# Output stage of three chunks with the weights held and 512 rows streamed, on one Trainium2 core

## The chip, the core and the metric

The kernel runs on one core of one Trainium2 chip. The metric is the device time of one launch in microseconds. Engines are named as in the profile: PE is TensorE's matmul stream and PEld its weight loads, DVE is VectorE, ACT ScalarE, POOL GpSimd, SP SyncE, which issues most DMAs.

## What is computed

One sequence of 2048 rows with 640 features, in bfloat16. The rows are normalised, and attention and a gated feed-forward block run side by side on the normalised rows; both are added to the input.

```python
xn = layernorm(x)                       # S=2048, D=640
q, k, v = split(xn @ wqkv)              # 32 heads of 20
s = q k^T * 20**-0.5, kept where 0 <= row - col < 256
o = softmax(s) v
h = sigmoid(xn @ w_gate) * (xn @ w_up)  # F=1536
out = x + o @ wo + h @ w_down
```

## The kernel before

**Tiling.** The rows are cut in four chunks of 512 (`CW`), a chunk into four blocks of 128 rows. Features lie in five groups of 128 (`DC`), the hidden 1536 in twelve (`FC`). Normalised rows are held turned (`xnT`, features on partitions). Gate and up products of a chunk give `h` (twelve tiles of 128 hidden features x 512 rows), attention gives `oc` (five tiles of 128 features x 512 rows).

**Order.** The schedule is by hand: every engine executes its instructions in the order in which the program names them. The main loop (`todo`) walks through 75 attention steps: scores on TensorE into one PSUM buffer of four banks (L504), the exponential on ScalarE (L510), masks on GpSimd (L493) and VectorE (L521), and two steps after the end of a pair the product with `v` (`pv`, L537), whose sums VectorE turns (L548), scales (L558, L563) and turns again into `oc` (L571). Between the steps the object `fill` draws pieces of the dense work from a list of generators: at least 1950 ns of it (`APART`) between two steps, and otherwise so much that a chunk's work is used up by its deadline. Every `yield` gives its nominal cost; most pieces also release one of the queued steps on VectorE (`fill.behind`). The list has, for each chunk, gate and up (`g_gu`, lines L418, L421, L427, L431), the projections (`g_qk`, `g_v`, lines L270, L274, L276, L328) and the output (`g_out`). `norms2` and `norms3` mix the normalising of later chunks in (L211, L230, L247).

**PSUM.** All dense work and `pv` share four banks (`ps_d`, tag "d"), handed out in turn.

**The output stage.** `g_out` runs for chunks 0, 1 and 2. For each block of 128 rows two accumulators take 12 matmuls each over the hidden features (`down`, L441: h is the stationary operand, 320 columns of `wd` stream), and then 5 each over `oc` (`add_wo`, L448). VectorE adds half of the sum to the rows of x (L452, the product with 0.5 because `h` and the ones in `v` carry a factor), and SyncE stores the block (L463). Loads of x (L458) are issued one block ahead into three buffers. Between the first block's `down` and its `add_wo` stands one gate/up group of the next work. Chunk 3's output is not in `g_out` but written out at the end of the kernel, with its four loads of x on ScalarE's queue.

**Neighbours on SyncE's queue.** In chunk 0 the loads of x stand ahead of the turn of chunk 2 (L252, L255), the spreading of q and k (L291) and x of chunk 3 (L118). Behind the stores come the writes of q and k of the next chunk (L278), each of them from one of six `st` buffers.

The weights' columns are taken at a step of five already in the projection of q and k:

```python
wt = wqkv[:, d, base:base + D].rearrange("p (k m) -> p m k", m=DC)
nc.tensor.matmul(ps, lhsT=wt[:, m, :], rhs=xnT[c][:, :, d, :], ...)   # L270
```

Of the kernel before, what the change touches and what calls it, by code (L numbers as in the profile page):

```python
# [9 lines left out]
P = 128  # L10
S = 2048
D = 640
# [3 lines left out]
DC = D // P  # L16
FC = F // P
CW = 512
NCH = S // CW
SBC = CW // P  # L20
HG = 4
# [8 lines left out]
ADD = mybir.AluOpType.add  # L30
MULT = mybir.AluOpType.mult
# [4 lines left out]
BF16 = mybir.dt.bfloat16  # L36
FP32 = mybir.dt.float32
# [32 lines left out]
def kernel(  # L70
# [11 lines left out]
    nc = tc.nc  # L82
    x2 = A_x.flatten_outer_dims()
    out2 = out.flatten_outer_dims()
    xr = x2.rearrange("(n p) d -> p n d", p=P)

    def pool(name, bufs, **kw):
        return ctx.enter_context(tc.tile_pool(name=name, bufs=bufs, **kw))

    const = pool("const", 1)  # L90
    xp = pool("xp", 1)
    lnp = pool("lnp", 4)
# [9 lines left out]
    tp = pool("tp", 2)  # L102
    np_ = pool("np", 1)
    ps_d = pool("ps_d", 4, space=bass.MemoryType.PSUM)
# [6 lines left out]
    xc = {}  # L111
# [12 lines left out]
    wd = const.tile([P, FC, D], BF16, name="wd")  # L124
    wo = const.tile([P, DC, D], BF16, name="wo")
# [208 lines left out]
    MM = 216  # L334
# [47 lines left out]
    def g_qk(c, behind={}):  # L382
        for w in "qk":
            for m in range(DC):
                proj_block(w, c, m)
                behind.get((w, m), lambda: None)()
                yield 5 * MM
        if c:
            spread("q", c, 0, 2)
            spread("k", c, 0, 2)  # L390
        else:
            for r in range(2):
                spread("q", c, r, r + 1)
                spread("k", c, r, r + 1)
                if r == 0:
                    load_gu(wu, B_w_up, 0, FS // 2)
# [11 lines left out]
    ht = {}  # L408
# [5 lines left out]
    def g_gu(c, f0, f1):  # L414
        for f in range(f0, f1):
            pg = ps_d.tile([P, CW], FP32, name="pg", tag="d")
            for d in range(DC):
                nc.tensor.matmul(pg, lhsT=part(wg, d, f), rhs=xnT[c][:, :, d, :],  # L418
                                 start=(d == 0), stop=(d == DC - 1))
            th = tp.tile([P, CW], FP32, name="th")  # L420
            nc.scalar.activation(out=th, in_=pg, func=TANH, scale=0.5)  # L421
            fill.hold = True
            yield 5 * MM
            fill.hold = False
            pu = ps_d.tile([P, CW], FP32, name="pu", tag="d")
            for d in range(DC):
                nc.tensor.matmul(pu, lhsT=part(wu, d, f), rhs=xnT[c][:, :, d, :],  # L427
                                 start=(d == 0), stop=(d == DC - 1))
            h = hp.tile([P, CW], BF16, name="h")
            ht[c, f] = h  # L430
            nc.vector.scalar_tensor_tensor(out=h, in0=th, scalar=1.0, in1=pu, op0=ADD, op1=MULT)  # L431
            yield 5 * MM


    oc = {}

    HALVES = ((0, HALF), (HALF, D))

    def down(c, s, y, cut):
        for f in range(FC):  # L440
            nc.tensor.matmul(y[:, 0:cut[1] - cut[0]], lhsT=ht[c, f][:, s * P:(s + 1) * P],  # L441
                             rhs=wd[:, f, cut[0]:cut[1]], start=(f == 0), stop=False)
            if f % 6 == 5:
                yield 6 * 136

    def add_wo(c, s, y, cut):
        for m in range(DC):
            nc.tensor.matmul(y[:, 0:cut[1] - cut[0]], lhsT=oc[c, m][:, s * P:(s + 1) * P],  # L448
                             rhs=wo[:, m, cut[0]:cut[1]], start=False, stop=(m == DC - 1))

    def add_x(y, cut, rows):
        nc.vector.scalar_tensor_tensor(  # L452
            out=rows[:, cut[0]:cut[1]], in0=y[:, 0:cut[1] - cut[0]], scalar=0.5,
            in1=rows[:, cut[0]:cut[1]], op0=MULT, op1=ADD)

    def new_rows(c, s, name="rows", bufs=3, queue=nc.sync):
        rows = lnp.tile([P, D], BF16, name=name, bufs=bufs)
        queue.dma_start(out=rows, in_=xr[:, c * SBC + s, :])  # L458
        return rows

    def store(c, s, rows, cut=(0, D), queue=nc.sync):
        sb = c * SBC + s
        queue.dma_start(out=out2[sb * P:(sb + 1) * P, cut[0]:cut[1]], in_=rows[:, cut[0]:cut[1]])  # L463

    def outp(c, s, ys, rows):
        for y, cut in zip(ys, HALVES):
            add_wo(c, s, y, cut)
        for y, cut in zip(ys, HALVES):
            add_x(y, cut, rows)
        store(c, s, rows)  # L470

    def g_out(c, between, ahead=()):
        coming = new_rows(c, 0)
        for s in range(SBC):
            rows = coming
            if s < SBC - 1:
                coming = new_rows(c, s + 1)
            if s == 0:
                yield from ahead
            ys = [ps_d.tile([P, CW], FP32, name=f"y{i}", tag="d") for i in range(2)]  # L480
            for y, cut in zip(ys, HALVES):
                yield from down(c, s, y, cut)
            if s == 0:
                yield from between
                fill.flush()
            outp(c, s, ys, rows)
            yield 10 * 136


    def select(part, n, sign):  # L490
# [125 lines left out]
    def mix(a, b, first, every=1, rest=True):  # L616

        for k, cost in enumerate(a):
            yield cost
            if k >= first and (k - first) % every == 0:  # L620
                yield next(b, 0)
        if rest:
            yield from b
# [94 lines left out]

    fill = Fill()
    GU = 10 * MM  # L720
    OUT = 4 * 34 * 136
    APART = 1950
    def later(load, *args):
        load(*args)
        yield 0
# [12 lines left out]
    fill.add("gu0c", mix(g_gu(0, 9, 12), norms2, 0, 1, False), 3 * GU)  # L738
    fill.add("gu1a", mix(g_gu(1, 0, 2), norms2, 0, 1, False), 2 * GU)
    fill.add("out0", mix(g_out(0, g_gu(1, 2, 3)), norms2, 1, 1), OUT + GU)  # L740
    fill.add("qk2", mix(g_qk(2), norms3, 2, 1, False), 50 * MM)
    fill.add("v2", g_v(2), 40 * 136)
    fill.add("gu1b", mix(g_gu(1, 3, 12), norms3, 0, 2), 9 * GU)
    fill.add("turn3", later(turn_rows, 3), 0)
    fill.add("out1", g_out(1, g_gu(2, 0, 1)), OUT + GU)
    fill.add("qk3", g_qk(3), 50 * MM)
    fill.add("v3", g_v(3), 40 * 136)
    fill.add("gu2", g_gu(2, 1, 12), 11 * GU)
    fill.add("out2", g_out(2, (), g_gu(3, 0, 1)), OUT + GU)
    fill.add("gu3", g_gu(3, 1, 12), 11 * GU)  # L750

# [34 lines left out]
    c = NCH - 1  # L786

    def run(gen):
        for _ in gen:
            pass  # L790

    rows = [new_rows(c, s, queue=nc.scalar) for s in range(SBC - 1)]
    rows.append(xp.tile([P, SBC, D], BF16, name="xc")[:, 0, :])
    nc.scalar.dma_start(out=rows[-1], in_=xr[:, S // P - 1, :])
    banks.close()
    ps_y = pool("ps_y", 4, space=bass.MemoryType.PSUM)
    ys = {}
# [53 lines left out]
```

## Time and profile before

| | us |
|---|---|
| median of 3 runs | 308.99 |
| lowest, highest | 308.94, 309.14 |
| profiled execution | 309.52 |
| span of that execution, first to last instruction | 307.2 |
| TensorE busy in it | 303.1 (99%) |
| ScalarE | 193.1 (63%) |
| VectorE | 184.2 (60%) |
| GpSimd | 83.4 (27%) |

The span is what the views of the profile cover; the time of the execution is longer by what lies around it. "Busy" counts an engine's instructions from start to end; matmuls are pipelined, so TensorE's share says that it is occupied, not that each of its cycles does work. The granted TensorE clock is 1.0 all through. The page has parts for busy time, for 40 slices of the span, for DMA queues, for the chain of work that ended last, and for groups of instructions. In a group's line stand: code line, engine, operation, out<-in, shape, count | busy us, mean ns of one | idle us of the engine before them, and what ended it.

### The profile page before, as it was taken

Reading aid. Unit: us, or ns where it says so; the run is one execution under the profiler, and the core shown is the slowest. Engines: PE = TensorE matmul, PEld = TensorE weight load, DVE = VectorE, ACT = ScalarE, POOL = GpSimd, SP = SyncE. Lnnn points to the kernel's source line nnn. Section 1 sums busy time; section 2 is a strip of 40 time slices with the busy share of each in tenths; the row PEclk is TensorE's granted clock in tenths of the full one; section 3 lists DMA queues with packets and bytes.
Section 4 is the critical chain, followed back from the end, with each engine's and each line's share of the span. In section 5 each row is a group of like instructions: output and inputs, shape, how many; then the busy total and the mean of one; then the engine's idle time right before and its main releaser. Section 6 shows DMA issues by size and latency. Waiting matters only on the chain.

```text
span 307.2 us, 10157 instructions
## 1 busy us (share of the span) xinstructions
PE 303.1 (99%) x4434; PEld 168.4 (55%) x4434; DVE 184.2 (60%) x378; ACT 193.1 (63%) x183; POOL 83.4 (27%) x189
## 2 busy tenths in 40 slices
PE   8999999999999999999999999999999999999996
PEld 3654445564556655654556655644546665444774
DVE  5777449298984489487642666354383627464523
ACT  6923795977766458867656557768765466778000
POOL 5011234635314123512213132341314132221100
PEclk9999999999999999999999999999999999999999
DMA  7998899789029522721052022550000210000301
GB/s 215 346 279 258 278 266 317 212 251 220 5 81 274 151 78 99 216 81 66 23 128 87 25 76 88 182 173 2 3 2 5 69 39 23 2 2 2 89 21 64
DMA packets 35756, 36.86 MB, mean 120 GB/s; under 512 B 2944, under 2 KB 35456, under 8 KB 35712
## 3 DMA queue, kind: packets, MB, share of 16 engines
q1 hardware_dynamic: 34304, 33.84, 37.2%
q0 software_dynamic: 544, 1.61, 1.7%
q10 hardware_dynamic: 864, 0.77, 0.9%
q8 instruction: 34, 0.56, 0.7%
q14 instruction: 10, 0.08, 0.1%
HBM read 25.59 MB, written 11.44 MB: 121 GB/s over the span
## 4 chain that ended last, share of the span: by engine, by line
PE 97%; DMA 1%; ACT 0%; DVE 0%; SPq 0%; issue 0%
PE pg L418 18%; PE y L441 18%; PE pu L427 17%; PE pqk L270 15%; PE ps L504 9%; PE y L448 7%; PE acc L537 6%; PE pv L328 6%; PE pv L308 1%; DMA xc<-in_A_x_dram 1%; PE pt L236 0%; PE pvh L308 0%; ACT turn L644 0%; PE pwarm L200 0%; DVE turn L230 0%; SPq L135 0%
## 5 line engine op out<-in xcount | busy, mean ns | idle before, releaser
L510 ACT ACTIVATE pT<-ps 128x2048 bf16<-128x2048 f32 x75 | 140.8, 1877 | 55.2 <-PE ps L504 32.6
L493 POOL TENSOR_SCALAR_AFFINE_SELECT pT<-pT 64x256 bf16<-64x256 bf16 (+1 forms) x126 | 67.2, 533 | 180.2 <-ACT pT L510 122.1
L418 PE MATMUL pg<-xnT,wg 128*128 128x512 bf16 x240 | 59.9, 380 | 0.0
L427 PE MATMUL pu<-xnT,wu 128*128 128x512 bf16 x240 | 59.8, 380 | 0.0
L431 DVE SCALAR_TENSOR_TENSOR h<-th,pu 128x512 bf16<-128x512 f32 x48 | 32.8, 684 | 42.4 <-ACT th L421 25.7
L441 PE MATMUL y<-wd,h 128*128 128x320 bf16 (+2 forms) x396 | 56.8, 295 | 0.0
L270 PE MATMUL pqk<-xnT,wqkv 128*128 128x512 bf16 x200 | 45.8, 381 | 0.0
L441 PEld LDWEIGHTS <-h 128*128 128x128 bf16 x396 | 36.8, 98 | 15.9 <-issue 2.3
L521 DVE TENSOR_TENSOR pT<-pT,keep 128x512 bf16<-128x512 bf16 (+2 forms) x81 | 35.5, 445 | 15.3 <-ACT pT L510 14.4
L421 ACT ACTIVATE th<-pg 128x512 f32<-128x512 f32 x48 | 28.6, 595 | 20.2 <-PE pg L418 19.9
L427 PEld LDWEIGHTS <-wu 128*128 128x128 bf16 x240 | 22.3, 98 | 27.3 <-issue 2.0
L418 PEld LDWEIGHTS <-wg 128*128 128x128 bf16 x240 | 21.7, 98 | 26.4 <-issue 3.0
L270 PEld LDWEIGHTS <-wqkv 128*128 128x128 bf16 x200 | 22.6, 119 | 19.0 <-issue 1.5
L504 PE MATMUL ps<-qT,kT 20*64 20x320 bf16 (+4 forms) x1440 | 32.0, 260 | 0.0
L548 DVE STREAM_TRANSPOSE t<-acc 128x512 f32<-128x512 f32 x32 | 21.0, 694 | 17.8 <-PE acc L537 17.8
L452 DVE SCALAR_TENSOR_TENSOR rows<-y,rows 128x320 bf16<-128x320 f32 x30 | 14.2, 488 | 25.2 <-PE y L448 20.4
L504 PEld LDWEIGHTS <-kT 20*64 20x64 bf16 x1440 | 13.5, 103 | 27.2 <-issue 27.1
L448 PE MATMUL y<-wo,oc 128*128 128x320 bf16 (+2 forms) x165 | 24.2, 295 | 0.0
L537 PE MATMUL acc<-pT,v 64*32 64x320 bf16 (+4 forms) x1440 | 20.0, 253 | 0.0
L448 PEld LDWEIGHTS <-oc 128*128 128x128 bf16 x165 | 15.5, 98 | 6.7 <-issue 1.0
L537 PEld LDWEIGHTS <-v 64*32 64x32 bf16 x1440 | 17.0, 92 | 3.4 <-issue 0.9
L328 PE MATMUL pv<-wqkv,xnT 128*64 128x320 bf16 x240 | 17.4, 300 | 0.0
(61 smaller groups left out, 174.1 us busy)
## 6 DMA issues: line engine op xcount, KB each, us to landing
qT<-sq SPq DMA_DIRECT2D x16, 256.0 KB, 4.4
kT<-sk SPq DMA_DIRECT2D x16, 256.0 KB, 4.3
xc<-in_A_x_dram SPq DMA_DIRECT2D x16, 160.0 KB, 4.3
sq<-st SPq DMA_DIRECT2D x20, 128.0 KB, 3.7
sk<-st SPq DMA_DIRECT2D x20, 128.0 KB, 2.8
out_dram<-rows SPq DMA_DIRECT2D x15, 160.0 KB, 1.8
wg<-in_B_w_gate_dram SPq DMA_DIRECT2D x4, 480.0 KB, 7.7
wu<-in_B_w_up_dram SPq DMA_DIRECT2D x4, 480.0 KB, 6.8
```

Source lines behind the costliest of these rows:

```text
L270: nc.tensor.matmul(ps, lhsT=wt[:, m, :], rhs=xnT[c][:, :, d, :], start=(d == 0), stop=(d == DC - 1))
L328: nc.tensor.matmul(ps[hf * U:(hf + 1) * U, 0:HALF], lhsT=xnT[c][:, s, d, rows], rhs=wqkv[:, d, 2 * D + hf * HALF:2 * D + (hf + 1) * HALF], ...
L418: nc.tensor.matmul(pg, lhsT=part(wg, d, f), rhs=xnT[c][:, :, d, :], start=(d == 0), stop=(d == DC - 1))
L427: nc.tensor.matmul(pu, lhsT=part(wu, d, f), rhs=xnT[c][:, :, d, :], start=(d == 0), stop=(d == DC - 1))
L431: nc.vector.scalar_tensor_tensor(out=h, in0=th, scalar=1.0, in1=pu, op0=ADD, op1=MULT)
L441: nc.tensor.matmul(y[:, 0:cut[1] - cut[0]], lhsT=ht[c, f][:, s * P:(s + 1) * P], rhs=wd[:, f, cut[0]:cut[1]], start=(f == 0), stop=False)
L448: nc.tensor.matmul(y[:, 0:cut[1] - cut[0]], lhsT=oc[c, m][:, s * P:(s + 1) * P], rhs=wo[:, m, cut[0]:cut[1]], start=False, stop=(m == DC - 1))
L493: nc.gpsimd.affine_select(out=part, in_=part, pattern=pattern, compare_op=GE, fill=0.0, base=-1 if sign > 0 else 0, channel_multiplier=sign)
L504: nc.tensor.matmul(ps[side * U:(side + 1) * U, i, col * U:(col + n) * U], lhsT=qk["k", kc, half][32 * i:32 * i + DH, 2 * r + side, kb * U: ...
L510: nc.scalar.activation(out=pt[:, :, 0:used, :], in_=ps[:, :, 0:used * U], func=EXP, scale=SCALE)
L521: nc.vector.tensor_tensor(out=part, in0=part, in1=limit.to_broadcast([P, HG, n * U]), op=MIN)
L537: nc.tensor.matmul(accs[side][32 * i:32 * i + 32, q * U:(q + n) * U], lhsT=vt[sb][rows, b, at:at + 32], rhs=pt[rows, i, col:col + n, :], s ...
```

## The change

For chunks 0 to 2 the output stage is turned round. A slice of 128 output features of `wd` or `wo` (every fifth column, so that partition p of the result is feature 5p + m) is the stationary operand, and `h` or `oc` with all 512 rows of the chunk streams. One accumulator `yT` holds 128 features x 512 rows; there are five of them a chunk, each with 12 + 5 matmuls. VectorE turns the accumulator by 32x32 blocks into an SBUF tile (from the pool of the gate's `th`), and adds half of it to x. x and the result lie in one tile per chunk: partition 32a + t holds rows t, 32 + t, ..., and of each row the 160 features of piece a. It is loaded by four DMAs at the start of the stage and stored by four at its end, in pieces of 160 features (320 B). The gate/up group stands now between the first accumulator's `wd` and `wo` matmuls. Chunk 3's output is as before, but takes its rows of x into the four slices of one tile (`xc`).

```diff
-    def new_rows(c, s, name="rows", bufs=3, queue=nc.sync):
-        rows = lnp.tile([P, D], BF16, name=name, bufs=bufs)
-        queue.dma_start(out=rows, in_=xr[:, c * SBC + s, :])
-        return rows
...
+    GW = D // HG
+
+    def by_feature(w, k, m):
+        return w[:, k, :].rearrange("p (j m) -> p m j", m=DC)[:, m]
+
+    def in_rows(dram, c):
+        return dram[c * CW:(c + 1) * CW, :].rearrange("(n t) (a e) -> a t n e", t=32, a=HG)
+
+    def new_chunk(c):
+        rows = lnp.tile([P, CW // 32, GW], BF16, name="rows", bufs=1)
+        for a in range(HG):
+            nc.sync.dma_start(out=rows[32 * a:32 * a + 32], in_=in_rows(x2, c)[a])
+        return rows
+
     def g_out(c, between, ahead=()):
-        coming = new_rows(c, 0)
-        for s in range(SBC):
-            rows = coming
-            if s < SBC - 1:
-                coming = new_rows(c, s + 1)
-            if s == 0:
-                yield from ahead
-            ys = [ps_d.tile([P, CW], FP32, name=f"y{i}", tag="d") for i in range(2)]
-            for y, cut in zip(ys, HALVES):
-                yield from down(c, s, y, cut)
-            if s == 0:
+        rows = new_chunk(c)
+        yield from ahead
+        for m in range(DC):
+            y = ps_d.tile([P, CW], FP32, name="yT", tag="d")
+            for f in range(FC):
+                nc.tensor.matmul(y, lhsT=by_feature(wd, f, m), rhs=ht[c, f], start=(f == 0), stop=False)
+                if f % 4 == 3:
+                    yield 4 * MM
+            if m == 0:
                 yield from between
                 fill.flush()
-            outp(c, s, ys, rows)
-            yield 10 * 136
+            for k in range(DC):
+                nc.tensor.matmul(y, lhsT=by_feature(wo, k, m), rhs=oc[c, k], start=False, stop=(k == DC - 1))
+            yt = tp.tile([P, CW], FP32, name="th")
+            nc.vector.transpose(out=yt, in_=y)
+            part = rows.rearrange("p n (i m) -> p m n i", m=DC)[:, m]
+            nc.vector.scalar_tensor_tensor(out=part, in0=yt.rearrange("p (n i) -> p n i", i=32), scalar=0.5, in1=part, op0=MULT, op1=ADD)
+            yield 5 * MM
+        for a in range(HG):
+            nc.sync.dma_start(out=in_rows(out2, c)[a], in_=rows[32 * a:32 * a + 32])
...
-    OUT = 4 * 34 * 136
+    OUT = 5 * 17 * MM
...
-    rows = [new_rows(c, s, queue=nc.scalar) for s in range(SBC - 1)]
-    rows.append(xp.tile([P, SBC, D], BF16, name="xc")[:, 0, :])
-    nc.scalar.dma_start(out=rows[-1], in_=xr[:, S // P - 1, :])
+    kept = xp.tile([P, SBC, D], BF16, name="xc")
+    rows = [kept[:, s, :] for s in range(SBC)]
+    for s in range(SBC):
+        nc.scalar.dma_start(out=rows[s], in_=xr[:, c * SBC + s, :])
```

## The prediction

> **What bounds the kernel now.** I read four views, from the coarse to the fine. First the page: who is busy, and which chain ended last.
>
> ```profile
> PE 303.1 (99%) x4434; PEld 168.4 (55%) x4434; DVE 184.2 (60%) x378; ACT 193.1 (63%) x183; POOL 83.4 (27%) x189
> ...
> PE 97%; DMA 1%; ACT 0%; DVE 0%; SPq 0%; issue 0%
> PE pg L418 18%; PE y L441 18%; PE pu L427 17%; PE pqk L270 15%; PE ps L504 9%; PE y L448 7%; PE acc L537 6%; PE pv L328 6%; PE pv L308 1%; DMA xc<-in_A_x_dram 1%; PE pt L236 0%; PE pvh L308 0%; ACT turn L644 0%; PE pwarm L200 0%; DVE turn L230 0%; SPq L135 0%
> ```
>
> TensorE is the chain: 97% of 307.2 us. The table of waits has no line in which a matmul waited for anything after the opening; the other engines wait for it. So the change is worth what it does to the sum of TensorE's steps, plus any wait that it newly puts into that row. Second, the chain in order of time:
>
> ```profile
> 13.16 10.79 PE pqk L270 x50
> ...
> 91.06 2.55 PE y L441 x18
> ...
> 102.23 1.63 PE y L441 x12
> ...
> 117.93 3.37 PE pqk L270 x15
> ...
> 189.69 2.29 PE pqk L270 x10
> ```
>
> Columns: start, length (us), work. A 512-wide matmul steps every 10.79/50 = 215.8 ns, a 320-wide one every 1.63/12 = 135.8 ns, each with a weight load of its own beneath it. A run that follows attention's small matmuls costs more: pqk x15 is 3.37 - 15 x 0.2158 = 0.13 us over, x10 2.29 - 2.16 = 0.13, y x18 2.55 - 18 x 0.1358 = 0.11. Third, the groups that keep shapes apart:
>
> ```profile
> L441 PEld LDWEIGHTS <-h 128*128 128x128 bf16 x396 | 36.8, 98 | 15.9 <-issue 2.3
> L270 PEld LDWEIGHTS <-wqkv 128*128 128x128 bf16 x200 | 22.6, 119 | 19.0 <-issue 1.5
> L431 DVE SCALAR_TENSOR_TENSOR h<-th,pu 128x512 bf16<-128x512 f32 x48 | 32.8, 684 | 42.4 <-ACT th L421 25.7 <-PE pu L427 16.8
> L548 DVE STREAM_TRANSPOSE t<-acc 128x512 f32<-128x512 f32 x32 | 21.0, 694 | 17.8 <-PE acc L537 17.8
> L452 DVE SCALAR_TENSOR_TENSOR rows<-y,rows 128x320 bf16<-128x320 f32 x30 | 14.2, 488 | 25.2 <-PE y L448 20.4 <-PE ps L504 2.6 <-DMA rows<-in_A_x_dram 2.2
> ```
>
> The load of L270 takes every fifth column (the slicing that the changed stage uses) and is 119 ns long; h's contiguous one is 98. The difference of 21 ns is the difference of the two excesses above: behind attention the first load is not hidden. Between the first and second matmul of such a run the trace's starts show 248 ns on L270 (32 over 216) in each of 12 runs, and 13 over on L418, L427, L441 and L448. Fourth, the stretches of the three output stages (82.0-107.7, 153.2-178.3, 246-272 us):
>
> ```profile
> 82.00:107.70 25.70, 25.70 (x411) 16.22 (x396) 16.22 (x33) 14.87 (x9) 6.48 (x12) 1.00 0.56 152
> 153.20:178.30 25.10, 25.10 (x384) 16.02 (x380) 11.88 (x24) 13.63 (x8) 5.24 (x10) 1.00 0.27 74
> ```
>
> Stretch, length, then PE, PEld, DVE, ACT, POOL busy: TensorE without a gap, VectorE 63% and 47%.
>
> **The change, part by part.** *Matmuls.* Each of chunks 0 to 2 loses 4 x 2 x 17 = 136 matmuls of 320 and gets 5 x 17 = 85 of 512: the same columns, 43520. Removed 408 x 0.1358 = 55.41 us, added 255 x 0.2158 = 55.03: -0.38 us, the fixed 2.5 ns of 153 matmuls.
>
> *Seams.* The order of instructions alternates dense and attention work as often as before. Entered from attention are 20 runs of the new stage, with strided weights, against 21 of the old in these chunks; the missing one is a gate run (13 over). Added 20 x (32 - 10.5) ns, 2.5 of the 13 being in every step already: +0.43 us. Together **+0.05 us**. [...]
>
> *VectorE.* Removed 24 x 0.49 = 11.8 us. Added 15 transposes of the f32 accumulator, the same form as L548, 0.694, and 15 additions. An addition reads f32 from SBUF and bf16 at a step of five: between 0.45 us (L521, 128x512, all bf16) and 0.83 (L563, strided, 517 ns for 320 elements, times 1.6); I take 0.69, nearest to L431. That is 20.8, so +9.0 us, 3.0 per stage: 19.2 of 25.7 us in the first, 60% in the others. All of it lies beside matmuls. Per 128 features TensorE brings 17 x 0.216 = 3.7 us plus attention; VectorE has 1.4 us plus one or two masks of 0.45, and once or twice a chunk a pair's finish (2 x 0.65 + 0.35 + 2 x 0.5 + 0.7 = 3.4). The accumulator is let go by the transpose alone, and comes up again four banks on. If that cover were gone, 9.0 us is the ceiling of the cost.
>
> *The wait for the last pair.* The output projection needs attention's last turned tiles. Chunk 0 is tightest: oc is ready at 87.5 us, L448 starts at 88.4. Now 12 wide matmuls (2.59) stand there for 24 narrow ones (3.26): it starts at 87.7, but oc's late pieces are the fourth and fifth operand, at 88.35. Margin 0.87 us; cost nothing.
>
> *Steps of the scores.* One PSUM buffer, 1.88 us of ACT. The pieces between two steps become 864, 864, 864, 1080 ns for 816 x4, 1360; since at least 1950 is always drawn, no gap is below 2160 (pu and the five wo matmuls in chunk 1, with a tanh ahead of the exponential on ACT). Gaps of 2160 with a tanh ahead stand in the old gate/up runs too (pg, scores, pu, pg, scores at 144.2 to 148.3 us), with no matmul waiting.
>
> *Transfers.* Per chunk 4 loads and 4 stores of 512 packets of 320 B instead of 128 of 1280 B. In the packet records 1280 B takes 55 ns, 256 B 18, 384 B 22; about 20 for 320: 2048 x 20/16 = 2.6 us for a chunk against 1.8. SyncE issues 512 packets (turn, 89.06) in 0.38 us, as 128 (0.43). Loads move to the head of the stage: chunk 0's past turn's write, which is 18 us later anyway. Stores move to the end, ahead of chunk 2's and 3's projections on the queue; these wait then for a transpose (0.7) and two more issues (0.4 each): 111.4 for 109.9. The first lands at 115.1 (3.7 us, the page's median), while the seventh st, which needs the first's buffer, comes at 117.6. In the tail the four loads keep their place on ACT's queue (283.5, used at 296.3): nothing.
>
> The sum, +0.05 us, is made on the profiled execution: 309.52 (span 307.2 and 2.3 around it) becomes 309.57. That execution lies 0.53 above the median of the runs, so 308.99 becomes 309.0.
>
> **The rivals.**
> - *The strided load hides after all* at the seams, in the wider matmul's shadow: -0.38, **308.6 us**. Against it: L270's matmuls are 512 wide and show the 32 ns.
> - *Slower: x comes late in chunk 1.* There SyncE stands until 152.9 for xnT's buffer, so the loads go out at 154.7 to 156.1. The first addition is wanted at 160.9: after 153.2 come 27 wide and gate/up matmuls (5.8), two score steps (0.9), a seam and the last matmul's end (0.3), and a transpose (0.7). If the data is not there VectorE stands, and behind it in its queue are two masks that the next pv reads at about 167.7 (56 such matmuls, 12.1 us, and five score steps with seams, 2.4). With 0.7 and 0.45 us of work in between, it decides at a landing 10.5 us after the last issue; from there every us is one on TensorE. The old loads land after 3.4 us, 6.7 at most. At a landing after 14 us (packets near 100 ns) the price is 3.5: **312.5**. [...]
> - *VectorE falls behind*: an addition of over 2 us instead of 0.69, so that masks and st copies come late. With half of the extra 9.0 us on TensorE: **313.5**. Against it: every 128x512 row of VectorE lies between 0.45 and 0.70.
> - *The wide stream starves on its strided loads*: at 230 instead of 215.8 ns, 255 x 14 = 3.6, **312.6**. Against it: pqk x50 in 10.79.
> - *Faster by more*: a wait of TensorE in the stage would have to vanish, and the stretches show none; one unseen us gives **308.0**.
>
> **How the numbers follow.** About 0.2% (0.6 us) is what a measurement of this kernel can tell from no change. Forecast 0.69; strided load hidden 0.11, still within that bound; late x 0.07, VectorE behind 0.06, starved stream 0.03, faster by more 0.04. So faster 0.04, same 0.80, slower 0.16. The range leaves out the last four (0.20): from 308.4, the hidden load less the spread of the runs (0.2), to 309.7, the forecast with the seams at twice their price (+0.43) and that spread.
>
> **What would show it.** Right: yT groups of TensorE at 215.8 ns a step, weight loads near 119 ns, the first step after attention at 248; TensorE at 97% of the chain; the transpose 0.69 and the addition 0.45 to 0.83; about 193 us of VectorE; no wait of acc for a mask. Wrong: the chain passes through rows' load or VectorE at 155 to 170 us, loads of rows that land after more than 10 us, score steps that wait for ACT, or a TensorE sum that differs by over 0.5 us.

## The result and the profile after

| | before | after |
|---|---|---|
| median, runs in turns on one chip | 309.07 us (308.94 to 309.74, 6 runs) | 310.70 us (310.41 to 312.04, 6 runs) |
| profiled execution | 309.52 | 310.59 |
| its span | 307.2 | 308.8 |

The ratio is 1.0052, 95% interval 1.0037 to 1.0068: 0.5% slower. The forecast was no difference, 309.0 us, 308.4 to 309.7. The page of the kernel after, with the lines that answer to those shown of before; one line of its queue table, the instruction queue's, is added because the answer hangs on it:

```profile
PE 301.6 (98%) x4267; PEld 159.0 (51%) x4281; DVE 205.1 (66%) x384; ACT 192.9 (62%) x183; POOL 85.3 (28%) x189
...
q8 instruction: 33, 0.54, 0.8%
...
PE 94%; DMA 3%; issue 1%; ACT 0%; DVE 0%; SPq 0%
```

TensorE is still the chain, but 94% of it for 97%: the rest is a DMA, and "issue", time in which it waited for nothing that the profile shows. VectorE is at 205.1 us where 193 were forecast. (4267 matmuls for 4281 weight loads: 14 matmul records are missing.) The groups name what changed on the way:

```profile
L487 PEld LDWEIGHTS <-wd 128*128 128x128 bf16 x180 | 20.0, 119 | 17.4 <-issue 2.5
...
L498 DVE SCALAR_TENSOR_TENSOR rows<-th,rows 128x512 bf16<-128x512 f32 x15 | 24.8, 1652 | 2.6 <-DMA rows<-in_A_x_dram 2.1
...
L496 DVE STREAM_TRANSPOSE th<-yT 128x512 f32<-128x512 f32 x15 | 10.6, 709 | 10.0 <-PE yT L494 10.0
```

The load of the weights (119 ns) and the transpose (709) are as forecast; the addition, forecast at 690 ns, takes 1652. The stretches of the first two output stages, columns as before (PE, PEld, DVE, ACT, POOL):

```profile
82.00:107.70 25.70, 24.92 (x378) 13.28 (x360) 22.74 (x36) 15.25 (x9) 5.12 (x11) 1.00 0.47 120
153.20:178.30 25.10, 24.50 (x317) 12.72 (x319) 17.39 (x26) 13.63 (x8) 6.23 (x10) 1.00 0.31 54
```

VectorE fills 88% of the first stretch. It would be easy to stop here and blame it. The table of TensorE's waits (total, times, longest, in us) says otherwise:

```profile
PE yT L487 <- issue: 1.3, 7, 0.2
PE pwarm L200 <- PEq L850: 0.8, 1, 0.8
PE yT L494 <- issue: 0.7, 4, 0.2
PE acc L551 <- issue: 0.6, 1, 0.6
PE pu L427 <- DMA wu<-in_B_w_up_dram: 0.5, 1, 0.5
```

The same table of the kernel before has two lines, both of the opening:

```profile
PE pwarm L200 <- PEq L835: 0.8, 1, 0.8
PE pt L236 <- DVE turn L230: 0.3, 1, 0.3
```

None of the lines of after names VectorE, and pwarm stands in both. The two yT lines are the missing matmul records: the weight loads, whose records are complete, run through at 216 ns there. Two real waits are left: 0.5 us for the up weights, at 32 us, far ahead of the first changed stage; and 0.6 us in acc. I laid the two traces over each other at the 75 score steps (counted from 0), which both kernels have in the same order, and took the difference of their times wherever the same work lies behind both:

| up to | TensorE later than before by | gained there |
|---|---|---|
| first score step, 31.5 us | 0.05 us | 0.05 |
| next score step, 35.7 us | 0.59 us | 0.54, wait for the up weights at 32.4 us |
| end of the three output stages, each against its start | | 0.02, 0.00, 0.02 |
| score step 46, 185 us | | 0.11 |
| inside pv of chunk 2's first pair, 204.3 us | | 0.82 |
| last matmul | 1.57 | |

The changed stages thus cost nearly nothing where they stand, as forecast. The largest item lies 26 us behind the end of the second stage (178.0 us) and 28 us ahead of the third (232.2 us). The chain in order of time shows it (start, length, work):

```profile
202.89 0.36 PE ps L518 x24
203.25 1.23 PE acc L551 x89
204.48 0.64 issue
205.12 0.21 PE acc L551 x3
205.33 0.75 PE pu L427 x3
```

Three matmuls ahead of its end, pv's run stops, and no semaphore is what starts it again.

**The theory, and its rival.** Queue q8 is taken to carry TensorE's own program: 33 transfers of 16,384 bytes each. The page of before has the same row:

```profile
q8 instruction: 34, 0.56, 0.7%
```

TensorE's 4281 weight loads and as many matmuls, divided by 33, are 259 instructions a transfer; before, 2 x 4434 by 34 are 261. I take 256 for the length of a piece; experiments 2 and 6 bear it out, with stops that lie whole pieces of 256 apart to within 0.03 of a piece. Counted so from the first weight load, this stop stands at 22.703 pieces. The packet records show a transfer of q8 starting at 202.80 us, 0.94 us long, and TensorE goes on 2.32 us after that start. Theory F (fetch): TensorE waits for the next piece of its program. One attention step and its pv, 24 + 96 matmuls with a load each, are 240 of the 256 instructions of a piece and run in 1.6 us; where a piece ends in such a burst, the next one is not there. The change made the program 306 instructions shorter, two thirds of that ahead of this place, and so moved the end of a piece to here. Theory S (stage): the rebuilt stage itself makes the loss, by VectorE's length, by the small packets of x and result, or by the strided weights.

### The profile page after: what moved, and what is told of

It is laid out like the page before. It is cut to its first block, busy times and chain, and to the rows that moved or that the text cites. A ratio compares the mean times of both kernels' runs of the same rounds, so it can differ in the third digit from the quotient of the medians.

```text
span 308.8 us, 9842 instructions
## 1 busy us (share of the span) xinstructions
PE 301.6 (98%) x4267; PEld 159.0 (51%) x4281; DVE 205.1 (66%) x384; ACT 192.9 (62%) x183; POOL 85.3 (28%) x189
## 4 chain that ended last, share of the span: by engine, by line
PE 94%; DMA 3%; issue 1%; ACT 0%; DVE 0%; SPq 0%
PE pg L418 16%; PE pu L427 16%; PE pqk L270 14%; PE yT L487 13%; PE ps L518 9%; PE acc L551 6%; PE pv L328 6%; PE yT L494 5%; PE y L441 4%; PE y L448 2%; DMA wu<-in_B_w_up_dram 1%; PE pv L308 1%; DMA xc<-in_A_x_dram 1%; DMA sk<-st 1%; PE pt L236 0%
## 5 line engine op out<-in xcount | busy, mean ns | idle before, releaser
L507 POOL TENSOR_SCALAR_AFFINE_SELECT pT<-pT 64x256 bf16<-64x256 bf16 (+1 forms) x126 | 69.0, 548 | 178.8 <-ACT pT L524 119.7
L431 DVE SCALAR_TENSOR_TENSOR h<-th,pu 128x512 bf16<-128x512 f32 x48 | 32.9, 685 | 42.1 <-PE pu L427 22.8
L487 PE MATMUL yT<-h,wd 128*128 128x512 bf16 x170 | 41.2, 381 | 1.4 <-issue 1.3
L535 DVE TENSOR_TENSOR pT<-pT,keep 128x512 bf16<-128x512 bf16 (+2 forms) x81 | 36.4, 460 | 6.8 <-ACT pT L524 6.1
L487 PEld LDWEIGHTS <-wd 128*128 128x128 bf16 x180 | 20.0, 119 | 17.4 <-issue 2.5
L498 DVE SCALAR_TENSOR_TENSOR rows<-th,rows 128x512 bf16<-128x512 f32 x15 | 24.8, 1652 | 2.6 <-DMA rows<-in_A_x_dram 2.1
L494 PE MATMUL yT<-oc,wo 128*128 128x512 bf16 x71 | 17.8, 379 | 0.7 <-issue 0.7
L496 DVE STREAM_TRANSPOSE th<-yT 128x512 f32<-128x512 f32 x15 | 10.6, 709 | 10.0 <-PE yT L494 10.0
```

Of the source, the lines that this page charges most:

```text
L487: nc.tensor.matmul(y, lhsT=by_feature(wd, f, m), rhs=ht[c, f], start=(f == 0), stop=False)
L494: nc.tensor.matmul(y, lhsT=by_feature(wo, k, m), rhs=oc[c, k], start=False, stop=(k == DC - 1))
L507: nc.gpsimd.affine_select(out=part, in_=part, pattern=pattern, compare_op=GE, fill=0.0, base=-1 if sign > 0 else 0, channel_multiplier=sign)
L535: nc.vector.tensor_tensor(out=part, in0=part, in1=limit.to_broadcast([P, HG, n * U]), op=MIN)
```

## Experiments

All runs were timed in turns with the kernel before, on the same chip. An experiment's trace is laid over that of before as above.

**1. The changed kernel again.**

> The changed kernel once more, nothing edited. In its first trace TensorE lost 1.57 us against before: 0.54 at 32 us (wu's second half lands late, before anything that the change touches), 0.82 at 204 us (in the middle of pv's matmuls, with no semaphore named), and 0.15 in the three output stages together. Theory F (instruction fetch): the 0.82 is a wait of TensorE for its own program, tied to where the 16 KB pieces of the program end, so it comes again at 204 us with 0.7 to 0.9 us; the 0.54 is a hazard of the opening and may differ by half a us either way. Theory S (the stage itself is slower: slow additions and small pieces of x): the loss should then show inside 82-108, 153-179 or 246-273 us, and the wait at 204 need not return. Time by both about 1.005 of before.

Measured: 310.53 us (310.01 to 310.86), before 309.26; ratio 1.0036 (1.0023 to 1.0050). In this execution the opening cost 0.02 us, the output stages 0.05, 0.00 and 0.03, step 46 again 0.11, and the stop was longer than expected, 1.31 us for 0.7 to 0.9, at the same instruction, 22.703. Its chain:

```profile
202.72 1.23 PE acc L551 x89
203.95 1.13 issue
205.07 0.21 PE acc L551 x3
```

So the wait for the up weights in the first execution belongs to that execution and not to the change; the stop belongs to the kernel.

**2. The program moved, in both kernels.** The matmuls at TensorE's very start (`warm`) are 36 narrow ones in place of 10 wide ones (4.00 us in the trace of a_shift52 for 4.43 in that of after); every instruction behind stands 52 later. The same edit goes into the kernel after (a_shift52) and before (b_shift52).

```diff
-            nc.tensor.matmul(ps, lhsT=ones[:, 0:P], rhs=ones, start=(k == 0), stop=(k == n - 1))
+            nc.tensor.matmul(ps[:, 0:w], lhsT=ones[:, 0:P], rhs=ones[:, 0:w], start=(k == 0), stop=(k == n - 1))
...
-    warm(10)
+    warm(36, P)
```

> The changed kernel with the ten warming matmuls of 512 columns at the start cut into 36 of 128: the same length at the opening's clock, but 52 instructions more in TensorE's program, so every later instruction lies 52 places further on and the ends of the 16 KB pieces (256 instructions) fall 52 instructions earlier in the code. Theory F: the wait of 0.82 us in the middle of the pv at 204 us goes, because the fetch then falls into the dense matmuls ahead; no other wait over 0.3 us takes its place; time 0.7 to 0.9 us under the changed kernel's of the same call. Theory S: nothing changes, within 0.2 us.

> The kernel before with the same 52 additional instructions at the start. At the pv of chunk 2's first pair its program then stands at the same place within a 16 KB piece as the changed kernel's at 204 us. Theory F with the position alone: a wait of TensorE of 0.5 to 0.9 us appears in that pv (at about 203.7 us), and the kernel becomes 0.5 to 0.9 us slower than before. Theory F with the position and the loads of x together (the fetch stands behind 2048 small packets there): a wait of 0 to 0.4 us. Theory S: same time as before.

Measured: a_shift52 309.57 us, ratio 1.0012 (1.0000 to 1.0024), and no stop. b_shift52 310.59 us, ratio 1.0045 (1.0028 to 1.0063): the kernel before, with nothing of the change in it, has the stop and the loss. The stop is 1.30 us, longer than the 0.5 to 0.9 that were expected. Its chain:

```profile
202.47 0.36 PE ps L504 x24
202.83 1.24 PE acc L537 x90
204.07 1.11 issue
205.18 0.20 PE acc L537 x2
```

Its piece ends at 23.703, and it is one piece longer (35 transfers). This alone speaks against theory S. The edit also touched the opening, which came 1.72 us later in the profiled execution of a_shift52 and 0.30 in that of b_shift52, so its times are blurred; experiment 4 moves the program in a cleaner way.

**3. Long packets.** The loads and stores of the changed stage take 5120 bytes of a row of memory at a time (which features and rows they are is left out).

```diff
-        return dram[c * CW:(c + 1) * CW, :].rearrange("(n t) (a e) -> a t n e", t=32, a=HG)
+        return dram[c * CW:(c + 1) * CW, :].rearrange("(a t n) d -> a t (n d)", a=HG, t=32)
```

> The changed kernel with x loaded and the result stored in rows of 5120 contiguous bytes per partition instead of 16 pieces of 320: the same bytes, tiles, waits and instructions on the engines. Left out: the place of x and of the result (each partition gets four whole rows of the chunk). Theory F with the loads' part: the fetch at 202.8 us no longer shares the DMA engines with 2048 packets, and the wait at 204 us shrinks from 0.82 to under 0.4 us. Theory F with the position alone: it stays at 0.7 to 0.9 us. Theory S: the output stages' 0.15 us go, nothing else.

Measured: 310.42 us, ratio 1.0035 (1.0024 to 1.0046), with a stop of 1.04 us at 22.703. While the fetch ran, 246 packets were moved beside it, in a_again 770; the stop was there with both, 1.04 and 1.31 us. The small packets are not the cause.

**4. The changed kernel, moved by 40, with the opening left alone.** 20 of chunk 0's gate and up matmuls are made as two halves of 256 columns.

```diff
+    def halves(ps, w, f):
+        for lo in (0, CW // 2):
+            for d in range(DC):
+                nc.tensor.matmul(ps[:, lo:lo + CW // 2], lhsT=part(w, d, f),
+                                 rhs=xnT[0][:, lo // P:lo // P + 2, d, :],
+                                 start=(d == 0), stop=(d == DC - 1))
...
+            if c == 0 and f < 2:
+                halves(pg, wg, f)
```

> The changed kernel, with the first 20 gate and up matmuls of chunk 0 (512 columns) made as 40 of 256 columns, so that everything behind them stands 40 instructions later in TensorE's program (20 matmuls and 20 weight loads more); the opening is left alone. Fetch theory (TensorE waits in the middle of pv of chunk 2's first pair for the next 16 KB of its own program): the boundary between two pieces falls elsewhere, so no matmul gap over 0.5 us near 204 us; 0.05 to 0.08 us of the output stages, 0.11 us at the scores near 184 us and about 0.05 us for the halved matmuls stay: 309.4 to 309.6 us where the kernel before has 309.26. Stage theory (the rebuilt stages themselves, their VectorE work or their transfers make the loss): 310.4 to 310.6 us, with the gap where it was.

Measured: 309.49 us, ratio 1.0006 (0.9995 to 1.0016): no difference that can be told from the kernel before, and 1.04 us less than a_again. The place of the stop in the chain, now without one:

```profile
202.44 0.36 PE ps L531 x24
202.79 1.26 PE acc L564 x92
204.05 1.19 PE pu L438 x5
```

At the end TensorE is 0.29 us later than before: 0.11 in the opening with the halves, 0.08 in the three output stages (0.03, 0.02, 0.03), 0.11 at step 46. Laid over a_again, weight load by weight load, it differs in one place by more than 0.08 us: the stop, -1.35. The changed stage is as it was, VectorE too (205.3 us), and the loss is gone. As the cause of the loss, theory S falls; what it could still explain is the 0.08 us, and the 0.11 at step 46, which the changed kernels alone show.

**5. The terms of the sum, one by one, on top of a_split.** Weight columns side by side (a_pack; the order of the output's features is left out):

```diff
-        return w[:, k, :].rearrange("p (j m) -> p m j", m=DC)[:, m]
+        return w[:, k, m * P:(m + 1) * P]
```

> a_split with the 128 weight columns of a step of the output stage taken side by side in place of every fifth (the order of the output's features is left out). Both theories: weight loads of the stage at about 98 ns in place of 119, the first step behind attention at 216 to 229 ns in place of 248; over 20 seams and runs 0.4 us less in the output stages, so 0.3 to 0.45 us under a_split if the seam term of the prediction is real, no difference if the strided load is hidden at the seams too.

```profile
L500 PEld LDWEIGHTS <-wd 128*128 128x128 bf16 x180 | 16.4, 98 | 20.3 <-issue 2.5
L507 PEld LDWEIGHTS <-wo 128*128 128x128 bf16 x75 | 6.9, 98 | 8.4 <-issue 0.6
```

Measured: loads at 98 ns, and the three stages now *gain* 0.13, 0.12 and 0.13 us on before, where in a_split they lose 0.08: 0.46 us between the two. The time was 309.09 us, 0.40 under a_split. (This execution had a stop of its own, 0.41 us, at 3.727 pieces, where a_split, with as many instructions, has none.) Against before the ratio is 1.0000 (0.9986 to 1.0014).

The addition on runs of 32 features side by side (a_add; the features' places are left out):

```diff
-            part = rows.rearrange("p n (i m) -> p m n i", m=DC)[:, m]
+            part = rows.rearrange("p n (m i) -> p m n i", m=DC)[:, m]
```

> a_split with the addition reading and writing runs of 32 features side by side in place of every fifth (the place of the features is left out). Fetch theory: the addition falls from 1.65 to about 0.69 us and VectorE's busy time from 205 to about 191 us, the 0.11 us at the scores near 184 us goes, and the time is 0.1 us under a_split or equal to it. Stage theory by VectorE's length: the time falls to 309.2 us or below while a_split stays at 310.5.

```profile
L511 DVE SCALAR_TENSOR_TENSOR rows<-th,rows 128x512 bf16<-128x512 f32 x15 | 11.1, 740 | 2.4 <-DMA rows<-in_A_x_dram 1.9
```

Measured: 309.39 us, ratio 1.0006 (0.9997 to 1.0015); the addition at 740 ns and VectorE at 193.7 us, and TensorE ends 0.27 us behind before for 0.29. VectorE's 12 us more were hidden. The 0.11 us at step 46 did *not* go, against what I expected: the exponential ahead of it starts late in this kernel too, 0.35 us behind the last semaphore that it waits for (0.07 in before), and the cause is open. Three records of 761 to 1103 ns raise the mean to 740; the other twelve take 691 to 712.

What makes the addition long, in five forms of it in one kernel (a_probe; what is stored is left out):

```diff
+            apart = rows.rearrange("p n (i m) -> p m n i", m=DC)[:, m]
+            four = rows[:, :, 0:128].rearrange("p n (i m) -> p m n i", m=4)[:, 0]
+            two = rows[:, :, 0:64].rearrange("p n (i m) -> p m n i", m=2)[:, 0]
+            turned = yt.rearrange("p (n i) -> p n i", i=32)
+            flat = ht[c, 0].rearrange("p (n i) -> p n i", i=32)
+            to, part = ((apart, apart), (turned, apart), (apart, flat), (four, four), (two, two))[m]
```

> a_split with the five additions of each output stage in five forms (what is stored is left out): m=0 reads and writes every fifth feature, m=1 reads every fifth and writes side by side (FP32), m=2 reads side by side and writes every fifth, m=3 reads and writes every fourth, m=4 every second. If the read with a step is what is slow, m=1 stays near 1.65 us and m=2 near 0.69; if the write is, the other way round; if both add up, 1.1 to 1.2 us each. By the step: if the price grows with the bytes passed over, step 4 near 1.4 us and step 2 near 0.9; if any step costs the same, 1.65 us for all. The time of the whole is of no interest.

```profile
L516 DVE SCALAR_TENSOR_TENSOR rows<-th,rows 128x512 bf16<-128x512 f32 x9 | 11.5, 1275 | 2.0 <-DMA rows<-in_A_x_dram 1.8
...
L516 DVE SCALAR_TENSOR_TENSOR rows<-th,h 128x512 bf16<-128x512 f32 x3 | 4.8, 1610 | 0.1
...
L516 DVE SCALAR_TENSOR_TENSOR th<-th,rows 128x512 f32<-128x512 f32 x3 | 2.7, 892 | 0.1
```

Reading h side by side and writing every fifth feature takes 1610 ns; reading every fifth and writing side by side 754 and 756 ns in two of its three instructions, 1165 in the first, so the write is the price, and the read shows none beside a write in FP32 (the cause of the first one's length is open). The first line mixes three forms; apart, its records are 1617, 1687 and 1985 ns for step five, 1305 to 1327 for step four and 736 to 758 for step two.

**6. The theory as a rule, on the kernel before.** The kernel before was moved by 20, 40 and 80 instructions, as in experiment 4, and the place and size of a stop were forecast from its trace by the rule that the piece ending near 204 us lasts 5.0 us at least. (In the four executions with a stop there so far it lasted 4.6 to 5.1 us.)

> The kernel before, with 10 of chunk 0's gate and up matmuls made as 20 halves: 20 instructions more ahead of the place, none changed behind it. In the four runs with the gap the piece of 256 instructions that ends there (at 0.703 of a piece) lasts 5.0 us with the gap, and would have lasted 3.7 us without it. Fetch theory, as a rule in numbers: the piece that ends near 204 us cannot last under about 5.0 us. By the trace of before its 256 instructions, moved by 20, take 4.42 us (202.11 to 206.53 us), so a gap of about 0.6 us is expected near 206.5 us, in gate and up matmuls (pg or pu) and not in pv. Stage theory: no gap, since this kernel has no stage of the new kind. Time by the first theory 309.9 us, by the second 309.3.

> The same with 20 matmuls halved, 40 instructions more. By the trace of before the piece takes 3.45 us (200.92 to 204.37 us). Fetch theory: a gap of about 1.5 us near 204.4 us, in the gate or up matmuls right behind pv; time 310.8 us. Stage theory: no gap, 309.4 us.

> The same with 40 matmuls halved, 80 instructions more. By the trace of before the piece takes 3.91 us (199.48 to 203.40 us). Fetch theory: a gap of about 1.1 us near 203.4 us, inside pv, some 14 matmuls earlier in it than in the run with 52 more; time 310.5 us. Stage theory: no gap, 309.5 us.

Measured: 309.70 us (ratio 1.0020, 1.0004 to 1.0036), 311.16 (1.0060, 1.0038 to 1.0081) and 309.35 (1.0023, 0.9998 to 1.0047), before 309.17. The kernel moved by 40 has two stops. In its chain, first chunk 1 and then the place that was forecast, in the up matmuls behind pv:

```profile
131.88 1.19 PE acc L550 x83
133.07 0.99 issue
134.06 0.32 PE acc L550 x8
```

```profile
203.91 1.26 PE acc L550 x92
205.16 0.97 PE pu L438 x4
206.13 0.44 issue
206.57 0.39 PE pu L438
```

The second was forecast at 1.5 us and is 0.61 us net; the first, 1.26 us, was not forecast. The kernel moved by 20 has no stop near 206.5 but one of 0.3 us in the pv near 133 us; the one moved by 80 none in pv, and 0.16 us at 102 us. Of the ten executions of that last kernel four took 310.2 to 312.7 us and six 309.0 to 309.4; the traced one took 309.28, so what the four lost is not shown. The rule for the size fails. The place does not:

| kernel | stop at (pieces of 256 instructions) | lost there, us |
|---|---|---|
| after, a_again, a_long | 22.703 | 0.82, 1.31, 1.04 |
| b_shift52 | 23.703 | 1.30 |
| b_split40 | 14.711 and 23.703 | 1.26 and 0.61 |
| b_split20 | 14.711 | 0.3 |
| a_pack | 3.727 | 0.41 |
| b_split80 | 10.719 | 0.16 |

Every stop of 0.1 us or more that was found behind the opening stands at the same fraction of a piece, 0.70 to 0.73, whatever instruction lies there: pv, scores, or gate and up. That is a bound of the program, not of the work. In all nine of these stops (the table's first row holds three) TensorE goes on 2.2 to 3.1 us after a transfer of q8 has started, and that transfer is the first for 8.8 us or more. Counted from the transfer's end the time is narrower, 1.2 to 1.6 us, and it is a floor: with transfers and piece ends numbered from one (an end at the fraction of the nearest stop), at none of the 425 piece ends of the 13 traces does TensorE pass end n less than 1.2 us after the end of transfer n. The nine stops lie at that floor, with only two other piece ends among them. So TensorE waits for that transfer, and what the size of a stop depends on is when it starts, here 1.4 to 4.1 us after TensorE has passed the end of the piece before; in the quick piece without a stop in b_split80 (3.9 us) it started 0.6 us after. What sets that start was not found, and so the sizes could not be forecast.

## Why the prediction was wrong

**The step that failed is the first one: "So the change is worth what it does to the sum of TensorE's steps, plus any wait that it newly puts into that row."** The second half of that sentence was looked for in semaphores and transfers of data, in the stages that change, and all rivals were of that kind. TensorE's stream also waited for its own instructions (0.82 us in after), in a place that the change does not touch. Nothing in the text counts instructions: that 153 matmuls fewer mean 306 instructions fewer, and so another cut of the program, is not in it. The row was on the page of before (34 transfers of the instruction queue), and TensorE's waits there have no such line: at each piece end the transfer had ended 1.8 us before or more. Its price here is 0.82 to 1.31 us in executions of the changed kernel; the loss between the medians is 1.27 and 1.63. The same kernel moved by 40 instructions runs in 309.49, inside the range that was given. The predicted chance of 0.16 for slower thus met a mechanism that it was not made of.

Step by step:

- *Matmuls and seams*, +0.05 us: right. The stages cost 0.04 to 0.08 us in three executions. The seam term, +0.43, was taken away by itself in a_pack and measured 0.46. The trace shows 216 ns a step and 248 for the first one behind attention. In a_pack, with packed loads, that first step takes 226. The rival in which the strided load hides at the seams, with -0.38 for the sum, does not hold here: a packed load is 21 ns shorter (98 for 119), and the first step behind attention 22 (226 for 248).
- *The third stretch* that the prediction names, 246 to 272 us, is not the third stage: in the trace of before L441 and L448 of chunk 2 run from 230.7 to 253.6 us. No term of the sum was read from it.
- *VectorE*: hidden, as said, but mis-sized. The addition was taken at 0.69 us from L431 with bounds of 0.45 and 0.83, and measures 1.65. The rows that bounded it write features side by side or in runs of 20; none writes at a step. 15 x 0.96 us is 14.4, and VectorE stands at 205.1 us for 193. The rival "VectorE falls behind" asked for an addition of over 2 us, and this is close, yet nothing of it reached TensorE: a_add shortens it by 0.9 us and the time moves by 0.10.
- *The wait for the last pair, and the scores' steps*: nothing was forecast; 0.11 us came at one score step, from a late exponential, cause open.
- *Transfers*: no cost to TensorE, as said. A packet of 320 B took 28 ns (median), not about 20. The loads of x land after 2.3 to 7.6 us, not the 10.5 from which the rival decided; VectorE waits for them once, 2.1 us up to 163.1 us in chunk 1, where the rival had put it, and TensorE not at all. For its bytes the short packet took longer (320 B in 28 ns, 1280 B in 55), and the time does not show it: with 5120 B in a_long it was the same within its interval, 310.42 us for a_again's 310.53.
- *Strided stream starves; faster by more*: neither was seen.
- *The profiled execution*: 0.54 us of its 1.57 are a wait for the up weights that a_again does not have. Without the second execution it would have been put down to the change.

A version that beats both kernels was not found. a_pack shows what the idea can bring when the weights need not be read at a step: the stages gain 0.38 us on before, which is 0.12% and below what can be told here, and bringing the features into that order would have to be paid for elsewhere.

## What to carry to other kernels

Here an edit that took 306 instructions from TensorE, busy for 99% of the span, also moved the ends of the pieces in which its program is fetched, and a loss of 0.82 to 1.31 us appeared 26 us behind the nearest changed stage. After an edit that changes the number of instructions on so busy an engine, look for "issue" in its waits and see whether it stands at a fixed fraction of 256 instructions, here 0.70 to 0.73. Before such a loss is put down to the edit, move the program by some tens of instructions, in both kernels; here that turned 310.53 into 309.49 us, and 309.17 into 311.16. And bound a strided write of VectorE by a row that writes at that step, not by one of the same shape (1.65 us here, 0.69 to 0.71 in most records of a_add, which writes side by side).

## What the runs showed of the hardware

- *TensorE's program was fetched in pieces, and TensorE reached the end of a piece before the next one was in.* 96 matmuls and 96 loads of pv run in 1.26 us, 6.6 ns an instruction; where the fetch of the next piece started late, TensorE stood for 0.2 to 1.3 us, until 2.2 to 3.1 us after that start and 1.2 to 1.6 us after the transfer's end. Queue q8 moved 16,384 bytes a transfer, 33 transfers in after, 34 in before and 35 in b_shift52, and every stop lies at one fraction of 256 instructions, 0.70 to 0.73. In these nine stops the fetch was not hidden.
- *VectorE's write at a step.* 512 bf16 elements a partition from FP32: 0.69 to 0.71 us side by side in most records of a_add, 0.74 to 0.76 at a step of two, 1.31 to 1.33 at four (a_probe), 1.60 to 1.62 at five in most; a read at a step of five cost nothing that shows (0.75 with an FP32 write, in two of three records of a_probe).
